# Casting DMAs for q and k, four units ahead, and transposes as pairs of 64x64 tiles, in an attention and spectral-mixing kernel

## The chip, the cores and the metric

The kernel runs on one core of one Trainium2 chip. The metric is the device time of one execution in microseconds (us), and lower is better. Before the change it was 457.25 us (median of 3 runs, 457.01 to 457.38). PE is the matmul engine (PEld are its weight loads), DVE the vector engine, ACT the scalar engine and POOL the GpSimd engine. SP is the engine that issues plain DMAs here. A run over 1.5% above the fastest of its kernel counts as slow.

## The reference

```python
# attention: 8 batches, 8 heads, 576 tokens, head size 64, window 128, ALiBi bias
scores = q @ k.T / sqrt(64);  mask = (rel >= 0) & (rel < 128)      # rel = query position - key position
scores = where(mask, scores - slope[h] * |rel|, -1e9)
x = softmax(scores) @ v                    # heads side by side: x is [8, 576, 512]
# spectral mixing
X = rfft(x, axis=1)[:, :64]                # 64 modes are kept
Y[m] = X[m] @ (w_r[m] + 1j * w_i[m])       # 2 x 64 matrices of 512 x 512 fp32, 134 MB in all
u = x + irfft(Y, n=576)
out = u + relu(u @ w_ch)                   # [8, 576, 512] fp32
```

## The kernel before

Attention runs as 16 units of four heads. It is a software pipeline: one `STAGE` list fixes, for each engine, the order of the instructions of several units. After every second unit the forward transform ("spectrum") of one batch follows. The 128 mixing matrices of 1 MB are a long DMA stream. Some are loaded as bf16 by casting GpSimd DMAs while attention still runs (`AHEAD`, `LATER`), the others as fp32 by SP. After the last matrix, the inverse transform and the output remain.

```python
TPP = 9
STAGE = (
    ("exp", 1, 0), ("score", 0, 0), ("exp", 0, 0), ("value", 0, 1), ("spectrum", None, 2),
    ("cast", "v", 0), ("score", 2, 0), ("channels", None, 2), ("transpose", "k", -1),
    ("cast", "k", -2), ("exp", 2, 0), ("norm", 0, 1), ("cast", "q", -3), ("score", 3, 0),
    ("mask", 1, 0), ("value", 1, 1), ("evacuate", "k", -1), ("mask", 0, 0), ("exp", 3, 0),
    ("transpose", "q", -2), ("evacuate", "q", -2), ("score", 1, -1), ("norm", 1, 1),
)
# ... in load(u, w): v by three SP DMAs with rows of 512 B; q and k with rows of 2304 B:
            t = self.raw[w][:, u % 2]
            nc.sync.dma_start(
                out=t.rearrange("p e j d -> p e (j d)"),
                in_=src.rearrange("(e h) (p j) d -> (h p) e (j d)", h=2, j=TPP))
# ... in cast(u, w): DVE makes bf16 of it
            dst = self.mid.tile([P, TPP, 2, D], BF16, tag=w, name=w)
            nc.vector.tensor_copy(dst.rearrange("p j e d -> p e j d"), src)
        self.load(w, u + 2)
# ... in transpose(u, w)
        for j in range(TPP):
            nc.tensor.transpose(tp[:, j], src[:, j].rearrange("p e d -> p (e d)"), self.ident)
# ... in evacuate(u, w): PSUM to SBUF
        (self.nc.vector.tensor_copy if u < 2 and w == "q" else self.nc.scalar.copy)(
            dst.rearrange("q h (p j) -> q h p j", j=TPP), ...)
# ... in value(u, e): one PSUM buffer for the unnormalized output
        av = self.ps.tile([P, 2, 512], FP32, tag="av", bufs=1)     # (cut: the last one has another)
# ... in norm(u, e): DVE frees it
        nc.vector.reciprocal(rec, tiles[:, :, :, D])
        nc.vector.tensor_tensor(out=self.x[...], in0=tiles[...], in1=rec..., op=ALU.mult)
# ... the early weights, one stage after another, gated on that stage's x
    AHEAD = {0: 1, 1: 1, 2: 1, 4: 1, 5: 1, 7: 1, 8: 1, 10: 1, 11: 1, 12: 1, 13: 3, 14: 1}
    LATER = {14: 3, 15: 3}
    EARLY, NWA, NWB, AGAIN = 14, 6, 2, 8
```

The softmax here doesn't subtract the row's maximum and nothing guards it: scores larger than these inputs give would overflow.

Of the kernel before, what the change touches and what calls it, by code (L numbers as in the profile page):

```python
# [10 lines left out]
FP32 = mybir.dt.float32  # L11
BF16 = mybir.dt.bfloat16
# [8 lines left out]
P = 128  # L21
D = 64
# [5 lines left out]
FULL = 4  # L28
TAIL = 64

TPP = 9

W = D + 2

# [3 lines left out]
STAGE = (  # L38
    ("exp", 1, 0), ("score", 0, 0), ("exp", 0, 0), ("value", 0, 1), ("spectrum", None, 2),
    ("cast", "v", 0), ("score", 2, 0), ("channels", None, 2), ("transpose", "k", -1),  # L40
    ("cast", "k", -2), ("exp", 2, 0), ("norm", 0, 1), ("cast", "q", -3), ("score", 3, 0),
    ("mask", 1, 0), ("value", 1, 1), ("evacuate", "k", -1), ("mask", 0, 0), ("exp", 3, 0),
    ("transpose", "q", -2), ("evacuate", "q", -2), ("score", 1, -1), ("norm", 1, 1),
)
# [2 lines left out]
class _Scratch:  # L47


    def __init__(self, ap):  # L50
        self.ap, self.used, self.tags = ap, 0, {}
# [55 lines left out]
class _Attention:  # L107


    def __init__(self, tc, ctx, q, k, v, consts, x, XC, raw):  # L110
        self.tc, self.nc = tc, tc.nc
        self.q, self.k, self.v = q, k, v
        self.ident, self.F, self.FT = consts
        self.x, self.XC = x, XC
        B, H, S, _ = q.shape
        self.S, self.NG = S, H // 4
        self.units = [(b, g) for b in range(B) for g in range(self.NG)]
        self.raw = raw
        self.mid = ctx.enter_context(tc.tile_pool(name="amid", bufs=2))
        self.ps = ctx.enter_context(tc.tile_pool(name="aps", bufs=1, space=PSUM))  # L120
        fix = ctx.enter_context(tc.tile_pool(name="afix", bufs=1))
        self.table = fix.tile([P, H, 2, 2 * P], BF16, name="mask")
        self.bias = fix.tile([P, H, 2, 2 * P], BF16, name="bias")
        self.vb = [fix.tile([P, 2, 4, 2, 2 * W], BF16, name=f"vb{i}") for i in range(2)]
        self.vt = [fix.tile([P, 4, 2, W], BF16, name=f"vt{i}") for i in range(2)]
        self.qkT = [fix.tile([P, 2, 2, (FULL + 1) * P], BF16, name=f"qkT{i}") for i in range(2)]
        self.att = [fix.tile([P, FULL * 8 * P + 64], BF16, name=f"att{i}") for i in range(2)]
        self.loaded, self.casted, self.open = {}, {}, {}

    def fixtures(self, i):  # L130
        nc = self.nc
# [66 lines left out]
    def load(self, w, u):  # L198
        nc = self.nc
        if u >= len(self.units):  # L200
            return
        b, g = self.units[u]
        hs = slice(4 * g, 4 * g + 4)
        if w == "v":
            t = self.raw[w][:, u % 2]
            sv = self.v[b, hs]
            for pair in range(2):
                nc.sync.dma_start(
                    out=t[:, pair],
                    in_=sv[:, 2 * pair * P : 2 * (pair + 1) * P].rearrange(  # L210
                        "h (p j) d -> p h (j d)", j=2),
                )
            nc.sync.dma_start(
                out=t[64:96, 2],
                in_=sv[:, FULL * P :].rearrange("h (p j) d -> p h (j d)", j=2),
            )
        else:
            t = self.raw[w][:, u % 2]
            src = (self.q, self.k)["qk".index(w)][b, hs]
            nc.sync.dma_start(  # L220
                out=t.rearrange("p e j d -> p e (j d)"),
                in_=src.rearrange("(e h) (p j) d -> (h p) e (j d)", h=2, j=TPP),
            )
        self.loaded[w, u] = t

    def cast(self, u, w):

        nc = self.nc
        src = self.loaded.pop((w, u))
        if w == "v":  # L230
            src = src.rearrange("p s h (j d) -> p s h j d", j=2)
            for half in range(2):
                row = slice(64 * half, 64 * half + 64)
                nc.vector.tensor_copy(  # L234
                    self.vb[u % 2][row, :, :, :, W * half : W * half + D], src[row, :2])
            nc.vector.tensor_copy(self.vt[u % 2][64:96, :, :, :D], src[64:96, 2])
        else:
            dst = self.mid.tile([P, TPP, 2, D], BF16, tag=w, name=w)
            nc.vector.tensor_copy(dst.rearrange("p j e d -> p e j d"), src)  # L239
            self.casted[u, w] = dst  # L240
        self.load(w, u + 2)

    def transpose(self, u, w):
        nc = self.nc
        src = self.casted.pop((u, w))
        if (u, w) == (0, "k"):
            tp = self.ps.tile([P, TPP, P], BF16, tag="sc", bufs=2, name="tp")
        else:
            tp = self.ps.tile([P, TPP, P], BF16, tag="tp", name="tp")
        for j in range(TPP):  # L250
            nc.tensor.transpose(tp[:, j], src[:, j].rearrange("p e d -> p (e d)"), self.ident)  # L251
        self.open[w, u] = tp

    def evacuate(self, u, w):
        tp = self.open.pop((w, u))
        dst = self.qkT[u % 2][:, "qk".index(w), :, : self.S]
        (self.nc.vector.tensor_copy if u < 2 and w == "q" else self.nc.scalar.copy)(  # L257
            dst.rearrange("q h (p j) -> q h p j", j=TPP),
            tp.rearrange("q j (h p) -> q h p j", h=2),
        )  # L260
# [137 lines left out]
def kernel(  # L398
# [10 lines left out]
    nc = tc.nc  # L409
    ctx.enter_context(tc.manual_schedule(engines=ALL | {SP}))  # L410
    B, H, S, _ = q.shape
    NM, DM, _ = moe_w_r.shape
    AHEAD = {0: 1, 1: 1, 2: 1, 4: 1, 5: 1, 7: 1, 8: 1, 10: 1, 11: 1, 12: 1, 13: 3, 14: 1}
    LATER = {14: 3, 15: 3}
    EARLY, NWA, NWB, AGAIN = 14, 6, 2, 8
    HM = NM // 2

    const = ctx.enter_context(tc.tile_pool(name="const", bufs=1))
# [6 lines left out]
    norm = const.tile([P, 1], FP32, name="norm")  # L425
# [3 lines left out]
        tc.tile_pool(name="w1", bufs=EARLY, side="right", reuse_waits="tile")  # L429
    )  # L430
    rawpool = actx1.enter_context(tc.tile_pool(name="raw", bufs=1, side="right"))
    raw = {w: rawpool.tile([P, 2, 2, TPP, D], FP32, name=w + "r") for w in "qk"}
    raw["v"] = rawpool.tile([P, 2, 3, 4, 2 * D], FP32, name="vr")
    spare = [raw[w][:, i].rearrange("p e j d -> p (e j d)") for w in "qk" for i in range(2)]
    vflat = raw["v"].rearrange("p u s h d -> p (u s h d)")
    spare += [vflat[:, 2 * DM * i :] for i in range(3)]
    spare = [t[:, : 2 * DM].bitcast(BF16).rearrange("p (a e) -> p a e", a=4) for t in spare]
    wq, homes, todo_w, again = {}, {}, list(range(2 * NM)), []

    def load_w(n, pool, bf16, chosen=None):  # L440


        for i in ([i for i in todo_w if i not in again][:n] if chosen is None else chosen):
            todo_w.remove(i)
            src = (moe_w_r, moe_w_i)[i % 2][i // 2].rearrange("(p a) e -> p a e", a=4)
            homes[i] = pool
            if bf16:
                t = spare.pop(0) if pool is None else pool.tile([P, 4, DM], BF16, tag="w", name="w")
                nc.gpsimd.dma_start(out=t, in_=src)
                wq[i] = [t[:, a] for a in range(4)]  # L450
            else:
                t = pool.tile([P, 4, DM], FP32, tag="w", name="w")
                nc.sync.dma_start(out=t, in_=src)
                wq[i] = [t[:, a].bitcast(BF16)[:, 1::2] for a in range(4)]

    with ExitStack() as actx:
        at = _Attention(tc, actx, q, k, v, (ident, F, FT), x, XC, raw)
        n = len(at.units)
        for w, u in (("q", 0), ("k", 0), ("q", 1), ("k", 1), ("v", 0), ("v", 1)):
            at.load(w, u)  # L460
        done = set()

        def run(name, arg, u):
            if 0 <= u < n and (name, arg, u) not in done:
                done.add((name, arg, u))
                getattr(at, name)(u, arg)
# [14 lines left out]
        next(table, None)  # L481
        at.fixtures(1)
        nc.gpsimd.memset(XC[:, 4 * NC * NM :], 0.0)
        run("cast", "q", 0)
        run("transpose", "q", 0)
        run("cast", "k", 0)
        run("transpose", "k", 0)
        run("evacuate", "q", 0)
        for h in (1, 3):
# [2 lines left out]
        run("score", 1, 0)  # L492
        for h in (0, 2, 1, 3):
            at.offset(h)
        run("cast", "q", 1)
        run("transpose", "q", 1)
        run("evacuate", "q", 1)
        run("score", 0, 0)
# [1 line left out]
        for h in (0, 2):  # L500
            at.decay(h)
        run("exp", 0, 0)
        run("cast", "k", 1)
        run("cast", "v", 0)
        side = {0: [(at.offset, 4), (at.offset, 6), (at.decay, 5), (at.offset, 5), (at.decay, 7),
                    (at.offset, 7), (at.decay, 4), (at.decay, 6)]}
# [1 line left out]
        for stage in range(min(lags), n + max(lags)):  # L508
            for name, arg, lag in STAGE:
                run(name, arg, stage - lag)  # L510
                if name in ("transpose", "exp") and side.get(stage):
                    for _ in range(1 + (name == "transpose")):
                        fn, h = side[stage].pop(0)
                        fn(h)
            if stage == 3:
                at.inverse_table()
            if stage in AHEAD:
                if stage:
                    b, g = at.units[stage - 1]
                    nc.gpsimd.tensor_copy(gate[:1, :1], x[:1, b, 0, 256 * g : 256 * g + 1])  # L520
                load_w(AHEAD[stage], early, True)
            if stage in LATER:
                load_w(LATER[stage], None, True)

    with ExitStack() as mctx:
# [115 lines left out]
        for g in range(NM // 4):  # L641
            acc = ps.tile([P, DM], FP32, tag="acc", bufs=2, name="acc")
            for i in range(8):
                m, ri = 4 * g + i // 2, i % 2
                w = wq[2 * m + ri]
# [9 lines left out]
                k = 8 * g + i  # L655
# [165 lines left out]
```

## Time and profile before

| what | before |
|---|---|
| time | 457.25 us |
| time of two units (spectrum to spectrum) in steady attention | 13.4 us |
| busy in such a stretch of 13.3 us | PE 12.5, DVE 12.7, ACT 12.7 us |
| last exp of attention starts | 124.3 us |
| last weight packet starts | 412.3 us |
| DMA holes up to 400 us | 3.5 us, 2.1 of them in the first 15 us |

A DMA hole is counted from the trace's packet records: whenever fewer than 16 packets are in flight, the missing share of 16 is lost time. The records do not say which of the 16 DMA engines carries a packet, so this count can only miss idle time, not invent it.

The page of the kernel before: its 40-slice rows for the DMA engines' busy tenths and their GB/s, its two large DMA queues (packets, MB, share of the engines' time), and the shares of the chain of waits that ended last.

```profile
DMA  8999999999999999999999999999999999990598
GB/s 280 324 332 309 303 264 314 312 290 254 212 303 316 311 314 314 344 399 424 422 418 422 423 421 419 420 421 422 420 420 419 421 421 419 420 373 4 219 332 276
q1 hardware_dynamic: 47280, 142.62, 81.3%
q0 software_dynamic: 4560, 15.21, 16.7%
DMA 53%; PE 25%; DVE 12%; ACT 4%; issue 3%; POOL 1%; ACTq 0%; DVEq 0%; POOLq 0%
```

The DMA engines are full from the first slice to the last weight. The GB/s of attention are lower than the 420 of the weight stream because its packets are small (by the prediction's fit of the packet records, an estimate, one of 512 B takes 29 ns and one of 8192 B 311) and because a casting DMA is counted by the bytes it writes (on the page 512 KB for a mixing matrix loaded by GpSimd, 1024 KB for one loaded by SP).

The table of windows of the kernel before, for two stretches of two units each. Columns: start and end, length, then busy us (and instructions) of each engine, granted clock, DMA share, GB/s.

```profile
core 0: us, PE busy (x) PEld busy (x) DVE busy (x) ACT busy (x) POOL busy (x), PEclk, DMA share, GB/s
54.40:67.70 13.30, 12.54 (x231) 9.67 (x229) 12.66 (x23) 12.72 (x15) 1.05 (x2) 1.00 0.99 255
67.70:81.10 13.40, 12.67 (x243) 9.79 (x240) 12.38 (x24) 12.73 (x15) 2.15 (x4) 1.00 1.09 308
```

Three compute engines are about 95% busy in the same stretch in which the DMA engines are full.

### The profile page before, as it was taken

What the parts mean: (1) busy time and instruction counts of PE and PEld (TensorE: products, weight loads), DVE (VectorE), ACT (ScalarE), POOL (GpSimd) and SP (SyncE); (2) the same over time, 40 slices, a digit from 0 to 9 for tenths busy, and PEclk for the clock granted to TensorE, in tenths of its full rate; (3) what the DMA queues carried; (4) which work ended last, traced back from release to release, by engine and by line L of the source; (5) the groups of instructions that cost most, each with busy time, mean ns of one, the idle gap of its engine ahead of it and who ended that gap; (6) DMA issues with size and microseconds to landing.
All of it is one profiled execution on the core that took longest, in us unless ns stands there. A gap on an engine that the chain in (4) does not pass through costs nothing.

```text
span 457.1 us, 7826 instructions
## 1 busy us (share of the span) xinstructions
PE 359.5 (79%) x3292; PEld 189.4 (41%) x3292; DVE 173.3 (38%) x314; ACT 154.3 (34%) x191; POOL 54.5 (12%) x86
## 2 busy tenths in 40 slices
PE   4787999999876545667566788998989788987892
PEld 3466776777653212222222243443333343433230
DVE  7889699998732101010010151211120211203674
ACT  5868799999800000000000011221111111104671
POOL 8510001012311100000000000000000000000561
PEclk9889899999999788555777799999999999999997
DMA  8999999999999999999999999999999999990598
GB/s 280 324 332 309 303 264 314 312 290 254 212 303 316 311 314 314 344 399 424 422 418 422 423 421 419 420 421 422 420 420 419 421 421 419 420 373 4 219 332 276
DMA packets 51874, 158.31 MB, mean 346 GB/s; under 512 B 3712, under 2 KB 22656, under 8 KB 39040
## 3 DMA queue, kind: packets, MB, share of 16 engines
q1 hardware_dynamic: 47280, 142.62, 81.3%
q0 software_dynamic: 4560, 15.21, 16.7%
q8 instruction: 25, 0.41, 0.4%
q14 instruction: 9, 0.07, 0.0%
HBM read 163.58 MB, written 9.44 MB: 378 GB/s over the span
## 4 chain that ended last, share of the span: by engine, by line
DMA 53%; PE 25%; DVE 12%; ACT 4%; issue 3%; POOL 1%; ACTq 0%; DVEq 0%; POOLq 0%
DMA w<-in_moe_w_i_dram 32%; DMA w<-in_moe_w_r_dram 12%; DMA vr<-in_moe_w_i_dram 7%; PE acc L648 7%; PE av L332 3%; PE my L623 2%; DVE vb L234 2%; DVE x L348 2%; DMA qr<-in_q_dram 2%; DVE att L306 2%; PE tp L251 1%; DVE q L239 1%; PE yy L752 1%; PE xt L369 1%; PE warm L636 1%
## 5 line engine op out<-in xcount | busy, mean ns | idle before, releaser
L648 PE MATMUL acc<-w,XC 128*32 128x512 bf16 x488 | 143.6, 448 | 55.0 <-DMA w<-in_moe_w_r_dram 33.2
L648 PEld LDWEIGHTS <-XC 128*32 128x32 bf16 x512 | 59.7, 140 | 130.5 <-issue 98.8
L295 ACT ACTIVATE att<-sc 128x1024 bf16<-128x1024 f32 x64 | 64.1, 1032 | 8.9 <-PE sc L285 8.9
L629 ACT CAST XW<-my 128x512 bf16<-128x512 f32 x36 | 21.1, 585 | 110.2 <-PE my L587 110.2
L733 POOL TENSOR_TENSOR r<-r,x 128x1024 f32<-128x1024 f32 x8 | 17.1, 2132 | 272.7 <-ACT r L731 272.6
L571 ACT CAST ZW<-zw 128x512 bf16<-128x512 f32 x4 | 2.3, 585 | 135.6 <-PE zw L566 135.6
L543 DVE TENSOR_SCALAR yq<-acc 128x512 bf16<-128x512 f32 x14 | 9.7, 690 | 101.2 <-PE acc L648 101.2
L611 DVE COPY xT<-tr 128x1024 bf16<-128x1024 bf16 x18 | 12.4, 691 | 90.6 <-PE tr L609 90.6
L332 PE MATMUL av<-vb,att 128*128 128x132 bf16 (+1 forms) x576 | 39.2, 220 | 5.5 <-DVE x L348 3.6
L332 PEld LDWEIGHTS <-att 128*128 128x128 bf16 x704 | 37.4, 100 | 11.0 <-DVE x L348 8.0
L623 PE MATMUL my<-wch,xT 128*64 128x512 bf16 x288 | 37.9, 385 | 0.8 <-DVE xT L611 0.8
L257 ACT COPY qkT<-tp 128x1152 bf16<-128x1152 bf16 x30 | 33.5, 1116 | 2.8 <-PE tp L251 2.2
L285 PE MATMUL sc<-qkT 64*64 64x256 bf16 (+2 forms) x640 | 25.7, 269 | 2.1 <-ACT qkT L257 1.2
L348 DVE TENSOR_TENSOR x<-av,rec 128x640 bf16<-128x640 f32 x32 | 26.4, 824 | 1.1
L766 DVE TENSOR_TENSOR o<-yy,r 128x1024 f32<-128x1024 f32 (+1 forms) x20 | 21.7, 1114 | 8.0 <-PE yy L752 4.2
L285 PEld LDWEIGHTS <-qkT 64*64 64x64 bf16 x640 | 14.8, 111 | 19.2 <-issue 16.2
L623 PEld LDWEIGHTS <-xT 128*64 128x64 bf16 x288 | 13.2, 109 | 22.6 <-issue 9.3
L234 DVE CAST vb<-vr 64x1024 bf16<-64x1024 f32 x32 | 22.3, 697 | 0.2
L272 PE MATMUL sc<-bias,ident 128*128 128x512 bf16 x64 | 20.4, 402 | 1.4 <-ACT att L295 1.4
L306 DVE TENSOR_TENSOR att<-att,mask 128x1024 bf16<-128x1024 bf16 x32 | 20.6, 684 | 0.0
L731 ACT ACTIVATE r<-mm 128x1024 f32<-128x1024 f32 (+1 forms) x19 | 17.7, 977 | 6.7 <-PE mm L587 6.5
L251 PE MATMUL tp<-ident,q 128*128 128x128 bf16 x144 | 11.9, 234 | 5.4 <-DVE q L239 5.4
(105 smaller groups left out, 326.0 us busy)
## 6 DMA issues: line engine op xcount, KB each, us to landing
w<-in_moe_w_i_dram SPq DMA_DIRECT2D x54, 1024.0 KB, 18.4
w<-in_moe_w_r_dram SPq DMA_DIRECT2D x46, 1024.0 KB, 18.5
qr<-in_q_dram SPq DMA_DIRECT2D x16, 576.0 KB, 8.6
kr<-in_k_dram SPq DMA_DIRECT2D x16, 576.0 KB, 9.0
vr<-in_v_dram SPq DMA_DIRECT2D x32, 256.0 KB, 7.7
w<-in_moe_w_r_dram POOLq DMA_DIRECT2D x15, 512.0 KB, 23.5
out_dram<-o SPq DMA_DIRECT2D x15, 512.0 KB, 4.3
w<-in_moe_w_i_dram POOLq DMA_DIRECT2D x7, 512.0 KB, 8.3
```

The lines of the kernel that those rows point to most:

```text
L234: nc.vector.tensor_copy(self.vb[u % 2][row, :, :, :, W * half : W * half + D], src[row, :2])
L257: (self.nc.vector.tensor_copy if u < 2 and w == "q" else self.nc.scalar.copy)(dst.rearrange("q h (p j) -> q h p j", j=TPP), tp.rearrange(" ...
L272: nc.tensor.matmul(sc[:, e], lhsT=self.ident, rhs=self.bias[:, hv].rearrange("p j n -> p (j n)"), start=True, stop=False, skip_group_check ...
L285: nc.tensor.matmul(sc[64 * half : 64 * half + 64, e, j * 256 + c0 : j * 256 + c0 + n], lhsT=qkT[row, 1, h, k0 + j : k0 + P : 2], rhs=qkT[r ...
L295: self.nc.scalar.activation(self.att[u % 2][:, kt * 8 * P : (kt + 1) * 8 * P], sc.rearrange("p e n -> p (e n)"), AF.Exp, scale=1.0 / math. ...
L306: nc.vector.tensor_tensor(out=rows, in0=rows, in1=self.table[:, heads], op=ALU.mult)
L332: nc.tensor.matmul(bank[:, qt * W : qt * W + rhs[j].shape[1]], lhsT=att[:, o : o + P], rhs=rhs[j], start=(n == 0 and j == 0), stop=(n == l ...
L348: nc.vector.tensor_tensor(out=self.x[:, b, :, cs].rearrange("p t (h d) -> p h t d", h=2), in0=tiles[:, :, :, :D], in1=rec.unsqueeze(-1).br ...
L623: nc.tensor.matmul(mm[ROWS[half]], lhsT=lhsT, rhs=wch[:, dt], start=(dt == 0), stop=False, skip_group_check=True,)
L629: nc.scalar.copy(XW[:, j, n], mm)
L648: nc.tensor.matmul(acc[32 * (i // 2) : 32 * (i // 2) + 32], lhsT=XC[:, c0 : c0 + 31 * NM + 1 : NM], rhs=w[a], start=(ri == 0 and a == 0), ...
L766: nc.vector.tensor_tensor(out=o[:, c], in0=yy[:, c], in1=r[:, c], op=ALU.add)
```

## The change: its intent, and the diff

Casting DMAs deliver bf16, so DVE need not cast q and k. A row of 4608 B holds 18 tokens instead of 9, which halves the number of packets. Loading four units ahead should hide the loads' latency (on the page before, 8.6 and 9.0 us in the median from the issue of a q or k load to its landing). With 64 channels per row, the transposes become 36 tiles of 64x64, in pairs of one tile from partitions 0 to 63 and one from 64 to 127. DVE gets back part of the freed time by evacuating q of even units. The saved buffer space holds two more early weights.

```diff
-TPP = 9
+TPP = 18
+DEPTH = 4
@@ STAGE
-    ("cast", "k", -2), ("exp", 2, 0), ("norm", 0, 1), ("cast", "q", -3), ("score", 3, 0),
+    ("exp", 2, 0), ("norm", 0, 1), ("score", 3, 0),
@@ load
-            t = self.raw[w][:, u % 2]
-            nc.sync.dma_start(
-                out=t.rearrange("p e j d -> p e (j d)"),
-                in_=src.rearrange("(e h) (p j) d -> (h p) e (j d)", h=2, j=TPP),
+            t = self.raw[w][:, u % DEPTH]
+            nc.gpsimd.dma_start(
+                out=t.rearrange("p j d -> p (j d)"),
+                in_=src.rearrange("h (p j) d -> (h p) (j d)", j=TPP),
             )
@@ transpose
         for j in range(TPP):
-            nc.tensor.transpose(tp[:, j], src[:, j].rearrange("p e d -> p (e d)"), self.ident)
+            for e in range(2):
+                row = slice(64 * e, 64 * e + 64)
+                nc.tensor.transpose(tp[row, j], src[row, j], self.ident[row, row])
+        self.load(w, u + DEPTH)
@@ evacuate
-        (self.nc.vector.tensor_copy if u < 2 and w == "q" else self.nc.scalar.copy)(
+        (self.nc.vector.tensor_copy if w == "q" and (u < 2 or u % 2 == 0) else self.nc.scalar.copy)(
@@ schedule of the early weights
-    AHEAD = {0: 1, 1: 1, 2: 1, 4: 1, 5: 1, 7: 1, 8: 1, 10: 1, 11: 1, 12: 1, 13: 3, 14: 1}
-    LATER = {14: 3, 15: 3}
-    EARLY, NWA, NWB, AGAIN = 14, 6, 2, 8
+    AHEAD = {0: 1, 1: 1, 2: 1, 3: 1, 4: 1, 5: 1, 6: 1, 7: 1, 8: 1, 9: 1, 10: 1, 11: 2, 12: 2, 13: 1}
+    LATER = {13: 2, 14: 2, 15: 3}
+    EARLY, NWA, NWB, AGAIN = 16, 5, 2, 8
@@ first loads
-        for w, u in (("q", 0), ("k", 0), ("q", 1), ("k", 1), ("v", 0), ("v", 1)):
+        for w, u in [(w, u) for u in range(DEPTH) for w in "qkv" if w != "v" or u < 2]:
             at.load(w, u)
# cut: the removed casts, the shapes of the buffers, the spare slots made from them
```

More of the change, by code (lines that the diff above doesn't have):

```diff
@@ L127, in __init__ @@
         self.att = [fix.tile([P, FULL * 8 * P + 64], BF16, name=f"att{i}") for i in range(2)]
-        self.loaded, self.casted, self.open = {}, {}, {}
+        self.loaded, self.open = {}, {}
     def fixtures(self, i):
@@ L228, in cast @@
         nc = self.nc
-        src = self.loaded.pop((w, u))
-        if w == "v":
-            src = src.rearrange("p s h (j d) -> p s h j d", j=2)
-            for half in range(2):
-                row = slice(64 * half, 64 * half + 64)
-                nc.vector.tensor_copy(
-                    self.vb[u % 2][row, :, :, :, W * half : W * half + D], src[row, :2])
-            nc.vector.tensor_copy(self.vt[u % 2][64:96, :, :, :D], src[64:96, 2])
-        else:
-            dst = self.mid.tile([P, TPP, 2, D], BF16, tag=w, name=w)
-            nc.vector.tensor_copy(dst.rearrange("p j e d -> p e j d"), src)
-            self.casted[u, w] = dst
+        src = self.loaded.pop((w, u)).rearrange("p s h (j d) -> p s h j d", j=2)
+        for half in range(2):
+            row = slice(64 * half, 64 * half + 64)
+            nc.vector.tensor_copy(
+                self.vb[u % 2][row, :, :, :, W * half : W * half + D], src[row, :2])
+        nc.vector.tensor_copy(self.vt[u % 2][64:96, :, :, :D], src[64:96, 2])
         self.load(w, u + 2)
@@ L244, in transpose @@
         nc = self.nc
-        src = self.casted.pop((u, w))
+        src = self.loaded.pop((w, u))
         if (u, w) == (0, "k"):
-            tp = self.ps.tile([P, TPP, P], BF16, tag="sc", bufs=2, name="tp")
+            tp = self.ps.tile([P, TPP, D], BF16, tag="sc", bufs=2, name="tp")
         else:
-            tp = self.ps.tile([P, TPP, P], BF16, tag="tp", name="tp")
+            tp = self.ps.tile([P, TPP, D], BF16, tag="tp", name="tp")
         for j in range(TPP):
-            nc.tensor.transpose(tp[:, j], src[:, j].rearrange("p e d -> p (e d)"), self.ident)
+            for e in range(2):
+                row = slice(64 * e, 64 * e + 64)
+                nc.tensor.transpose(tp[row, j], src[row, j], self.ident[row, row])
         self.open[w, u] = tp
+        self.load(w, u + DEPTH)
     def evacuate(self, u, w):
@@ L431 @@
     rawpool = actx1.enter_context(tc.tile_pool(name="raw", bufs=1, side="right"))
-    raw = {w: rawpool.tile([P, 2, 2, TPP, D], FP32, name=w + "r") for w in "qk"}
+    raw = {w: rawpool.tile([P, DEPTH, TPP, D], BF16, name=w + "r") for w in "qk"}
     raw["v"] = rawpool.tile([P, 2, 3, 4, 2 * D], FP32, name="vr")
-    spare = [raw[w][:, i].rearrange("p e j d -> p (e j d)") for w in "qk" for i in range(2)]
+    spare = [raw[w][:, 2 * i : 2 * i + 2].rearrange("p u j d -> p (u j d)")[:, : 4 * DM]
+             for i in range(2) for w in "qk"]
     vflat = raw["v"].rearrange("p u s h d -> p (u s h d)")
-    spare += [vflat[:, 2 * DM * i :] for i in range(3)]
-    spare = [t[:, : 2 * DM].bitcast(BF16).rearrange("p (a e) -> p a e", a=4) for t in spare]
+    spare += [vflat[:, 2 * DM * i : 2 * DM * (i + 1)].bitcast(BF16) for i in range(3)]
+    spare = [t.rearrange("p (a e) -> p a e", a=4) for t in spare]
     wq, homes, todo_w, again = {}, {}, list(range(2 * NM)), []
@@ L483 @@
         nc.gpsimd.memset(XC[:, 4 * NC * NM :], 0.0)
-        run("cast", "q", 0)
         run("transpose", "q", 0)
-        run("cast", "k", 0)
         run("transpose", "k", 0)
@@ L494 @@
             at.offset(h)
-        run("cast", "q", 1)
         run("transpose", "q", 1)
@@ L502 @@
         run("exp", 0, 0)
-        run("cast", "k", 1)
         run("cast", "v", 0)
```

## The prediction

> **What bounds the kernel now.** The 16 DMA engines. In the trace's packet records at least 16 packets are in flight nearly always from 6 to 409 us; only 50-60 us (92% filled) and 100-120 us (96 to 99%) have small holes, 1.3 us together. The chain of waits is 53% DMA. After 200 us the engines move 420 GB/s; in attention (60-113 us) source bytes come at about 358 GB/s, because packets are small. Compute there is close behind: in two-unit stretches of 13.38 us (table of windows) PE is busy 12.6, ACT 12.7, DVE 12.4. The last weight lands at 412 us; the 45 us after it are untouched. So only fewer engine-seconds of DMA, or different DMA holes, move the end.
>
> **Cost per packet.** A fit (an estimate) of packet counts in saturated 4 us stretches gives 29 ns for 512 B (v), 96 for 2304 B (q, k), 311 for 8192 B (weights), 309 for a casting packet of 8192 B source. Cost follows source bytes; casting is free; a packet has 11-12 ns of its own. [...]
>
> **What the change does.**
> 1. q and k: 8192 packets of 96 ns become 4096 of an estimated 180 ns (4608 B source): 49.1 to 46.1 us on 16 engines. Gain 3 us, maybe 4.
> 2. A weight in nearly every stage fills the later holes: gain 1 us.
> 3. Start: eight casting loads (0.53 us of GpSimd each, the first 1.2, as weight issues show) now precede GpSimd's 16.6 us of setup. Identity, tables and masks come 4.4 us later, and unit 4's loads wait for the end of setup, at 22 us, with data 3 us later (before: weight issued 17.3, first packet 20.5). The work queued at the start is an estimated 16 us, so the engines run dry from about 18 us, with only v of unit 2 in between: loss 3 to 4 us.
> 4. DVE loses 32 casts of 0.76 us and gains 7 evacuations of 1.36, which ACT loses (1.12 each). PE swaps 9 transposes 56 ns apart for 36 of 64 columns; 66-column neighbours start 29 ns apart, so 0.55 us if pairs overlap like the score matmuls (3 ns apart), 1.1 if not, against 0.5. All off the critical path: a unit with its weight needs an estimated 7.4 us of DMA, above the 6.7 of compute.
> 5. Weight slots 16+7 bf16 and 5+2 fp32, against 14+6 and 6+2: seven still queue 17 us of DMA. Neutral.
>
> **Sum:** -3.4 - 1.0 + 3.5: **456.3 us**, range 451.5 to 460.5. Faster by over 2%: 0.07; within 2%: 0.88; slower by over 2%: 0.05.
>
> **What would show it.** 4096 packets of 2304 B on the software queue, instead of 8192 on the hardware one; a DMA hole between 18 and 25 us and none later; transposes waiting for qr and kr, DVE and ACT with new idle; still 420 GB/s after 200 us and the 45 us tail; first exp and forward table 3 to 4 us later.
>
> **What would make it wrong.** If the start hole is filled, or casting packets cost well under 180 ns: 3 to 5 us faster. If paired transposes make PE the limit (over 7.4 us a unit), or GpSimd, which waits in order for transposes, gates and earlier landings, issues loads late: holes in attention, 0.5 to 1 us per unit slower. If the smaller fp32 pool drains DMA where early slots are re-used: a few us more.

The sum, -3.4 - 1.0 + 3.5 = -0.9 us, takes the 457.25 us of before to about 456.3. A packet's own 11 to 12 ns are an estimate from the fit's figures: 96 ns for 2304 B and 311 ns for 8192 B leave 11.9 ns for no bytes at all. That GpSimd waits in order is seen in the trace before, where it waited 86.8 us in 11 pieces for the norms that gate the weights.

## More of the kernel before

Part of the chain of waits of the kernel before between 66 and 96 us (start, duration, what):

```profile
75.38 0.76 DVE k L239
76.30 0.82 DVE x L348
77.12 0.67 DVE q L239
77.79 1.20 DVE att L306 x2
79.16 0.83 DVE x L348
80.04 1.23 PE av L332 x20
```

The norm (`x`, 0.83 us) frees the one PSUM buffer (PSUM is the memory that PE writes to) called `av`, and the next value matmuls follow at once (at 80.04 us; the norm ends at 79.99). Apart from the norm's own reciprocal, which needs the value matmuls of its unit, nothing that stands before `x` on DVE in this stretch waits for PE.

## The result, and the profile after

The time rose to 470.59 us (median of 4 runs, 469.29 to 471.78), against 457.13 us of the kernel before in the same rounds (455.38 to 457.38, 4 runs). The ratio is 1.0302, with a 95% interval of 1.0264 to 1.034: slower by 3%. Ratios here and below are the mean time of one kernel's fast runs over that of the other's fast runs of the same rounds, so they are not quite the ratio of the quoted medians.

| what | before | after |
|---|---|---|
| two units, spectrum to spectrum, in turn | 16.9, 13.4, 13.4, 13.4, 13.4, 13.3, 8.8 us | 27.1, 16.3, 16.3, 17.0, 17.0, 14.8, 9.0 us |
| first exp, last exp start | 10.3, 124.3 us | 15.0, 150.6 us |
| DMA holes up to 400 us | 3.5 us | 14.3 us |
| of these from 15 to 25, from 40 to 80, from 80 to 160 us | 0.0, 0.8, 0.5 | 2.5, 6.2, 3.3 |
| last weight packet | 412.3 us | 425.2 us |
| from the last weight to the end | 45 us | 43 us |

The page of the kernel after, the same lines:

```profile
DMA  8899898999999999999999999999999999990498
GB/s 186 178 210 221 167 203 162 218 227 172 238 197 213 303 314 304 318 350 409 422 421 421 420 421 422 420 420 422 420 419 422 422 417 423 420 415 37 155 343 310
q1 hardware_dynamic: 38144, 120.60, 66.0%
q0 software_dynamic: 9600, 26.22, 29.9%
DMA 49%; PE 30%; issue 8%; DVE 7%; ACT 3%; POOL 2%; ACTq 0%; DVEq 0%; POOLq 0%
```

The busy digits hardly moved, and the weight stream after attention still runs at 420 GB/s. The chain has moved: PE and "issue" have grown, DMA has shrunk. The last weight comes 12.9 us later, and this is the whole loss (the tail after it is even 1.5 us shorter). The holes grew by 10.9 us, which is most of it.

The table of windows of the kernel after, for two stretches of two units (columns as before):

```profile
65.70:82.00 16.30, 13.01 (x334) 10.74 (x337) 10.54 (x18) 11.69 (x13) 4.17 (x8) 0.96 0.87 177
98.30:115.30 17.00, 13.79 (x336) 11.45 (x339) 11.40 (x21) 12.15 (x14) 3.63 (x7) 0.90 0.98 190
```

DVE and ACT do have less to do than before, and PE 0.3 to 1.3 us more, but the stretches are 3 to 3.6 us longer: every compute engine now waits about 3 us or more. Attention had become bound by waits between engines, while its DMA queue ran dry. The granted clock of PE is also lower where PE waits (0.91 in the mean from 60 to 120 us, against 1.00 before). The question is which waits.

**First finding: v arrives late.** The chain of waits of the kernel after, between 25 and 50 us:

```profile
25.94 0.45 DVE x L347
26.38 21.49 DMA vr<-in_v_dram
47.90 0.42 DVE vt L236
48.35 0.23 DVE rec L346
48.60 0.84 DVE x L347
49.48 2.14 PE av L331 x24
```

One load of v took 21.49 us from its issue to its landing. The view of the DMA engines for the window of 26 to 48 us, with packets, MB and share of engine time of each queue:

```profile
DMA packets 3320, 4.82 MB, mean 219 GB/s; under 512 B 238, under 2 KB 1920, under 8 KB 3317
q0 software_dynamic: 1575, 3.91, 91.0%
q1 hardware_dynamic: 1742, 0.86, 17.4%
```

Two queues had work: GpSimd's (q0) with q, k and weights, and SP's (q1) with v alone. They moved about the same number of packets, 1575 and 1742. But a packet of v is 512 B, and one of the other queue holds 4608 or 8192 B of source. In the packet records of each 2 us between 30 and 44 us, where both queues had work throughout, there are likewise 112 to 169 data packets of v and 109 to 151 of the casting queue. From 44 to 46 us the casting queue has only 79, and v at once has 303. So while both queues had work, v got about every second packet of data, but over the window only 17.4% of the engines' time. (On SP's queue here every record with data is a row of 512 B.) By what rule an engine picks between the queues the trace does not show; these are counts. Four units of q and k plus a weight per stage kept the casting queue supplied. Before, q and k stood on the same queue as v and had smaller packets (2304 B).

**Second finding: DVE waits in front of the norm.** The chain of waits of the kernel after, at 60 us:

```profile
60.62 0.62 PE tp L249 x32
61.35 1.36 DVE qkT L256
62.87 0.84 DVE x L347
63.75 2.16 PE av L331 x20
65.91 1.72 PE xt L368 x20
```

PE transposes q, DVE evacuates it in 1.36 us, and only then comes the norm `x`, which frees the single `av` buffer for PE. In the trace DVE works in the order of `STAGE`, where the evacuation (61.35 us) stands before the norm (62.87 us). On ACT, which evacuated q before, the norm did not stand behind it. The same evacuation stands in the chain at 78.6, 111.6 and 128.6 us as well. The table of waits of the kernel after (what waits, for what: total us, times, longest):

```profile
POOL kr L222 <- PE tp L249: 35.6, 9, 6.8
PE av L331 <- DVE x L347: 18.9, 9, 6.9
DVE qkT L256 <- PE tp L249: 14.1, 7, 2.2
```

The third line is the evacuation waiting for PE (7 times). The second is PE waiting for the norm; its longest wait, 6.9 us, is the one for v of the first finding. The second line in the kernel before:

```profile
PE av L332 <- DVE x L348: 3.6, 7, 1.2
```

The first line is how the wait reaches DMA: the loads of k are issued one unit at a time, when PE has read the old buffer. Late compute therefore issues loads late, and the engines run dry.

**Third finding: pauses that no semaphore explains.** From 60 to 140 us the chain of the kernel after also has pieces called "issue", one of them 1.73 us long at 94.64 us. In the kernel before, there is no such pause inside a group of matmuls, apart from short gaps of 0.3 to 0.56 us at the same places in both kernels, which are not counted below.

### The profile page after: what moved, and what is told of

Its sections match the earlier page's. It is cut to its first block, busy times and chain, and to the rows that moved or that the text cites. A ratio compares the mean times of both kernels' runs of the same rounds, so it can differ in the third digit from the quotient of the medians.

```text
span 468.6 us, 9492 instructions
## 1 busy us (share of the span) xinstructions
PE 353.9 (76%) x4119; PEld 196.3 (42%) x4156; DVE 161.7 (34%) x289; ACT 147.1 (31%) x184; POOL 71.9 (15%) x123
## 4 chain that ended last, share of the span: by engine, by line
DMA 49%; PE 30%; issue 8%; DVE 7%; ACT 3%; POOL 2%; ACTq 0%; DVEq 0%; POOLq 0%
DMA w<-in_moe_w_r_dram 24%; DMA w<-in_moe_w_i_dram 20%; PE acc L644 9%; PE av L331 5%; DMA vr<-in_v_dram 5%; PE tp L249 3%; PE sc L284 2%; PE xt L368 2%; PE my L619 1%; DVE qkT L256 1%; DVE o L762 1%; DVE x L347 1%; PE warm L632 1%; PE sc L271 1%; PE yy L748 1%
## 5 line engine op out<-in xcount | busy, mean ns | idle before, releaser
L644 PE MATMUL acc<-w,XC 128*32 128x512 bf16 x484 | 137.0, 434 | 55.0 <-DMA w<-in_moe_w_r_dram 34.5
L625 ACT CAST XW<-my 128x512 bf16<-128x512 f32 x36 | 21.1, 586 | 109.7 <-PE my L583 109.7
L331 PE MATMUL av<-vb,att 128*128 128x132 bf16 (+1 forms) x576 | 40.0, 222 | 20.2 <-DVE x L347 18.9
L256 ACT COPY qkT<-tp 128x1152 bf16<-128x1152 bf16 x23 | 25.6, 1114 | 12.4 <-PE tp L249 12.4
L284 PEld LDWEIGHTS <-qkT 64*64 64x64 bf16 x640 | 15.6, 108 | 22.2 <-issue 17.8
L727 ACT ACTIVATE r<-mm 128x1024 f32<-128x1024 f32 (+1 forms) x19 | 17.7, 977 | 6.7 <-PE mm L583 6.5
L256 DVE COPY qkT<-tp 128x1152 bf16<-128x1152 bf16 x9 | 12.1, 1348 | 14.1 <-PE tp L249 14.1
L271 PE MATMUL sc<-bias,ident 128*128 128x512 bf16 x34 | 14.1, 426 | 2.4 <-ACT att L294 2.3
## 6 DMA issues: line engine op xcount, KB each, us to landing
w<-in_moe_w_r_dram SPq DMA_DIRECT2D x52, 1024.0 KB, 16.3
```

Of the source, the lines that this page charges most:

```text
L256: (self.nc.vector.tensor_copy if w == "q" and (u < 2 or u % 2 == 0) else self.nc.scalar.copy)(dst.rearrange("q h (p j) -> q h p j", j=TPP) ...
L271: nc.tensor.matmul(sc[:, e], lhsT=self.ident, rhs=self.bias[:, hv].rearrange("p j n -> p (j n)"), start=True, stop=False, skip_group_check ...
L284: nc.tensor.matmul(sc[64 * half : 64 * half + 64, e, j * 256 + c0 : j * 256 + c0 + n], lhsT=qkT[row, 1, h, k0 + j : k0 + P : 2], rhs=qkT[r ...
L331: nc.tensor.matmul(bank[:, qt * W : qt * W + rhs[j].shape[1]], lhsT=att[:, o : o + P], rhs=rhs[j], start=(n == 0 and j == 0), stop=(n == l ...
L625: nc.scalar.copy(XW[:, j, n], mm)
L644: nc.tensor.matmul(acc[32 * (i // 2) : 32 * (i // 2) + 32], lhsT=XC[:, c0 : c0 + 31 * NM + 1 : NM], rhs=w[a], start=(ri == 0 and a == 0), ...
```

## The experiments

Eleven kernels ran. The first four undo one part of the changed kernel each, or two; the next two add one part to the kernel before; the last five tell the remaining causes apart. All outputs were correct. Line numbers in the profiles shift by a line or two between the kernels. "Pauses" below is the summed time in attention in which PE stood still inside a group of matmuls without a wait for any semaphore, from the trace's instruction records, counted from the start of the matmul before to the start of the one after (so each includes some 0.2 us of work); all these pauses ended 1.2 to 1.6 us after a 16 KB packet of the instruction queue had landed.

### e1_evac_act: q evacuated by ACT again

```diff
-        (self.nc.vector.tensor_copy if w == "q" and (u < 2 or u % 2 == 0) else self.nc.scalar.copy)(
+        (self.nc.vector.tensor_copy if w == "q" and u < 2 else self.nc.scalar.copy)(
```

> The changed kernel with one part undone: q of units 2, 4, ... 14 is evacuated by ScalarE again (units 0 and 1 stay on VectorE). Theory B (the evacuation on VectorE stands ahead of the norm of the unit before, so the single value buffer comes free late and PE waits): two units take 13.4 to 14.5 us in place of 16.9 between 60 and 130 us, the DMA holes after 60 us (about 5.5 us in the changed kernel) shrink to under 1.5, and the time falls by 4 to 7 us, to 464 to 467. Theory A (v is starved by the queue of casting loads): the stall of about 8 us near 37-46 us stays, and the time falls by at most 2 us. Theory C (paired transposes are too dear for PE): no change, as PE does the same.

Measured: 466.96 us (465.2 to 468.11), ratio 1.0217 [1.0181, 1.0252], so 3.6 us less than the changed kernel. The two-unit times were 25.4, 17.0, 16.7, 13.8, 18.6, 15.5 and 9.0 us, not the steady short ones that the theory asked for. The pauses without a semaphore rose from 2.95 us to 13.1 us. The evacuation matters, but as soon as this wait was gone, another took much of its place.

### e2_v_pool: the later loads of v on GpSimd's queue

```diff
-                nc.sync.dma_start(          # both places of v's load
+                (nc.sync if u < 2 else nc.gpsimd).dma_start(
```

> The changed kernel with the v loads of units 2 and up issued by GpSimd as well, in one queue with q, k and weights (uncast, same packets). Theory A [...]: VectorE's wait for v near 37-46 us (8.3 us) vanishes, with it the DMA hole at 50-60 us (3.3 us), and the time falls by 3 to 8 us. Theory B (order of the evacuation on VectorE): two units still take 16.5 to 17 us after 60 us and the time falls by at most 4 us. If GpSimd's in-order issue is the limit (theory D), three more issues per unit make it slower.

Measured: 464.79 us (463.67 to 466.63), ratio 1.0176 [1.0142, 1.0211], 5.8 us less. The hole from 40 to 60 us is gone (0.0 instead of 3.3 us), and the first two-unit time fell from 27.1 to 19.5 us. The six loads of v for units 3 and 4 land 7.7 to 10.1 us after their issue, against 12.6 to 21.5 us in the changed kernel and 7.5 to 10.8 us before it: v no longer falls behind on a queue of its own beside one of large packets. But this run changed a second thing, which its expectation ("same packets") had not foreseen. In the packet records, v on this queue stands as records of 4096 B. They can be told from the weights' records of the same size by their duration (mostly 140 to 240 ns, against 320 to 340), and a fit that does so (an estimate) gives about 195 ns for one, against 219 to 232 ns for eight of 512 B. Over 2016 such records on 16 engines that is an estimated 3 to 5 us of DMA time saved. The holes up to 400 us shrank by only 1.3 us (14.3 to 13.0). So the end of v's starvation is shown, but how much of the 5.8 us is due to it is not: a large part can be cheaper packets. The others stayed at 16.3 to 17.5 us, with PE still waiting for the norm.

### e3_both: both of these

```diff
# the edits of e1_evac_act and e2_v_pool together
```

> e1 and e2 together. If A and B are the two causes, nothing but the start hole is left: 458 to 462 us, DMA filled over 97% from 25 to 150 us, two units in 14 to 15 us (limited by loads). If the paired transposes or the casting packets (theory C) cost time, it stays above 464.

Measured: 461.38 us (459.2 to 463.23), ratio 1.0082 [1.0032, 1.0133]. The gain of 9.2 us is about the sum of the two (3.6 and 5.8). PE's wait for the norm fell from 18.9 to 1.2 us. But the two-unit times were still 21.1, 17.8, 17.7, 14.0, 17.8 and 13.8 us. A part of the chain of waits of this kernel:

```profile
64.30 0.59 PE tp L249 x30
64.89 2.88 issue
67.77 0.22 PE tp L249 x2
```

PE stops after 30 of 36 transposes of one group. The chain shows no other engine in this pause of 2.88 us. A packet of the instruction queue, 16384 B, started at 64.99 us and took 1.25 us; the transposes went on 1.53 us after it had landed. The pauses of this kernel sum to 14.3 us; the longest is 3.07 us. Counted in PE instructions (matmuls and weight loads), the pauses stand whole multiples of 256 apart: exactly so in e5_many_instr below (256 and 11 x 256), and to within 4 here, where the trace lacks some records. The count of packets of the instruction queue gives about as many instructions to each (32 packets for some 8314, 25 on the page of the kernel before for 6586, 28 in e7_both_wide for 7162); such 256 are called a block below. So the pauses lie one or more whole blocks apart and end after a packet has landed: from this the author infers that PE stands at the end of a block and waits for the next. No record shows that wait itself. This brought up a new theory: PE's own instruction stream, now longer by 27 transposes per q or k, does not come fast enough. The program has 8314 PE instructions, against 6586 before the change.

### e4_start: a shorter start, in the changed kernel

```diff
-        for w, u in [(w, u) for u in range(DEPTH) for w in "qkv" if w != "v" or u < 2]:
-            at.load(w, u)
+        for u in range(2):
+            at.load("v", u)
...      # q and k of units 0 and 1 are issued after the forward table's first POOL work,
...      # those of units 2 and 3 before fixtures(0); fixtures(1) moves behind the first transposes
```

> The changed kernel with its start reordered: GpSimd makes the identity and the index tables first, then loads units 0 and 1, then the distances, then loads units 2 and 3; q and k of unit 4 are issued before the second set of memsets. Start theory (4 to 5 us of casting issues ahead of GpSimd's setup delay everything and open a DMA hole at 15-25 us of 2.5 us): first exp 3 to 4 us earlier, hole under 0.7 us, time falls by 2 to 3 us. If A and B hold alone, the saved time at the start is lost again in the stall for v, and the time falls by under 1 us.

Measured: 470.04 us, ratio 1.0287 [1.0238, 1.0336]: nothing gained. The start itself worked: the hole from 15 to 25 us went from 2.5 to 0.0 us and the first exp from 15.0 to 12.6 us. But the holes from 40 to 80 us grew from 6.2 to 8.8 us. This fits an attention that is bound by its own waits: DMA work done earlier then only means that the queue is empty for longer later.

### e5_many_instr and e6_few_instr: more instructions, or the same PE time in few, in the kernel before

The first adds 27 transposes of 64x64 to each group of the kernel before (their results are overwritten). The second does the 9 transposes twice.

```diff
# e5_many_instr
+        for i in range(27):
+            row = slice(64 * (i % 2), 64 * (i % 2) + 64)
+            nc.tensor.transpose(tp[row, i // 2 % TPP, :D], src[row, i // 2 % TPP, 0], self.ident[row, row])
# e6_few_instr
+        for j in range(TPP):
+            nc.tensor.transpose(tp[:, j], src[:, j].rearrange("p e d -> p (e d)"), self.ident)
```

> The kernel before, with 27 extra transposes of 64x64 in front of the nine of each transpose call (their result is overwritten, so the output is right): PE executes as many instructions as in the changed kernel (8314 in the program, from 6586), in some 0.5 us of extra PE time per call. Theory D ([...] the PE stalls of e1_evac_act and e3_both end 1.2 to 1.6 us after such a block has landed): PE gaps of this kind of at least 5 us in all between 20 us and the end of attention (before: none), and two units take 15.5 us or more in place of 13.4. Rival (PE time, not instructions): no such gaps, two units in 14 to 15.4 us, the same as in e6_few_instr.

> The control: the kernel before with the nine 128x128 transposes of each call done twice (0.5 us of extra PE time per call, as much as in e5_many_instr, but a third of its extra instructions; 7162 in the program). Theory D: PE gaps after a block's landing under 2 us in all, two units in 14 to 15 us, faster than e5_many_instr. Rival: the same as e5_many_instr within 1 us of total time.

(Cut from the first: theory D's clause on how blocks would arrive and why one would come late, a conjecture then; "such a block" is a 16384 B packet of the instruction queue.)

Measured: 471.78 us, ratio 1.0313 [1.0279, 1.0347] for many, and 468.69 us (6 runs), ratio 1.0262 [1.0232, 1.0292] for few. Two units took 15.5 and 15.2 us, against 13.4. The pauses were only 2.7 us with many and none with few: the theory's forecast of 5 us or more was a miss. Two things differ from e3_both, the time per block and the packets of q and k, which are half as large here. As for the first: in this form the extra instructions come with extra PE time, so a new block of 256 is needed less often: an estimate from the counts and times is every 5.7 us here and every 5.2 in e3_both without its pauses, against 7.1 in the kernel before.

The control was the surprise. About 2.0 us more PE work per two units, with no other edit, made two units 1.8 us longer and the kernel 11.5 us longer. PE time in attention was hardly off the critical path even before the change.

### e7_both_wide: e3_both with 18 transposes instead of 36

The rows go back to 9 tokens, still cast by GpSimd DMAs and four units ahead. Each transpose takes all 128 partitions and 64 columns.

```diff
-TPP = 18
+TPP = 9
-                in_=src.rearrange("h (p j) d -> (h p) (j d)", j=TPP),
+                in_=src.rearrange("(e h) (p j) d -> (h p) e (j d)", h=2, j=TPP),
-                row = slice(64 * e, 64 * e + 64)
-                nc.tensor.transpose(tp[row, j], src[row, j], self.ident[row, row])
+                nc.tensor.transpose(tp[64 * e : 64 * e + 64, j], src[:, e, j], self.ident)
# cut: the shapes that go with it
```

> e3_both with q and k loaded as half rows (2.3 KB source, two per partition, still casting, still four units ahead) and transposed by 18 tiles of 128x64 in place of 36 of 64x64 (7162 PE instructions in place of 8314; 8192 q and k packets in place of 4096, 3 us more of DMA time). Theory D: the PE stalls after a block's landing (about 15 us in all in e3_both) fall under 4 us, two units take 14 to 15.5 us, attention ends 5 us or more earlier than in e3_both; the total gains 2 to 4 us net of the dearer packets, 457 to 460. Without theory D it is 2 to 4 us slower than e3_both.

Measured: 456.18 us (455.08 to 457.3), ratio 0.9976 [0.9946, 1.0005]. The pauses are gone (0), two units take 13.7 us throughout after the first 18.1, and there is no DMA hole after 25 us. Against e3_both this is 5.2 us, more than the forecast of 2 to 4. By the trace one group takes PE 0.474 us instead of 0.563. With four groups in two units that is 0.4 us, too little for the 4 us by which e3_both's long stretches exceed 13.7. PE's granted clock from 60 to 120 us is back at 1.00.

This run does not separate the number of instructions from the size of the packets, since the rows became half as long too. A count of PE's instructions in the traces (an estimate) lets one look at both. From the start of one block to the landing of the next it takes at most 4.4 us here, 5.4 in e5_many_instr and 6.7 in e3_both. So a block also came sooner here. Whether the shorter rows (2304 B of source a packet instead of 4608) are the reason was not shown. Many instructions with short rows and no extra PE time were not run.

### e8_all_wide: e7_both_wide with the start of e4_start

```diff
# the edit of e4_start on e7_both_wide
```

> e7_both_wide with the reordered start of e4_start. With the other three causes gone, the start hole should count at last (it gained nothing in e4_start, because the time was lost again in the waits for v): 2 to 4 us faster than e7_both_wide, 454 to 457, and DMA holes of under 5 us in all up to 400 us. If the start does not matter, the same as e7_both_wide within 1 us.

Measured: 453.04 us (452.54 to 453.27), ratio 0.9905 [0.9882, 0.9929]. This version beats the kernel before by 1%, and the changed one by about 4%. The same edit that gained nothing in e4_start is worth 3.1 us here. The page of this kernel, the DMA rows and the chain:

```profile
DMA  8999999999999999999999999999999999980598
GB/s 170 196 201 237 245 234 244 235 242 242 237 220 317 315 317 315 351 404 424 422 422 420 421 420 420 420 422 418 422 420 420 420 422 418 421 335 4 207 340 293
DMA 54%; PE 26%; issue 6%; POOL 6%; ACT 4%; DVE 3%; ACTq 0%; DVEq 0%; SPq 0%; POOLq 0%
```

The holes sum to 3.9 us, as before the change (3.5), and the last weight comes at 407.3 us, 5.0 us before that of the kernel before. A fit says where that can come from (an estimate, with v's and the weights' records told apart as in e2_v_pool): a casting q or k packet of 2304 B source costs about 93 ns here (96 in e11_wide_v_sp, where v is on the other queue), and the same bytes on SP's queue cost 96 to 98 ns before, so 8192 of them save 0 to 3 us. The joined records of v save another 3 to 5 us. So much of the gain over the kernel before can be due to v's larger packets, which are no part of the change, and not to casting.

### e9_no_weights: e3_both with no early weights until late

All 16 early weights are loaded at stage 13, so that during attention the DMA engines have little to do. This was one run with a profile; its state is unknown, so only what happens inside attention is read from it.

```diff
-    AHEAD = {0: 1, 1: 1, 2: 1, 3: 1, 4: 1, 5: 1, 6: 1, 7: 1, 8: 1, 9: 1, 10: 1, 11: 2, 12: 2, 13: 1}
+    AHEAD = {13: 16}
```

> e3_both with all sixteen early weights loaded at stage 13 in place of one or two per stage, so that the DMA engines are far from full in attention; PE's instructions stay the same (8314 in the program). It must be slower in total (about 30 us of weight loads come later). Theory D [...]: PE stalls inside a group of matmuls after a block's landing fall from about 14 us in all (e3_both) to under 3 us, and two units take about 14.0 us between 60 and 110 us (e3_both: 17.8, 17.7, 14.0, 17.8). If the number of instructions alone makes PE stall, whatever the DMA engines do, the stalls stay at 10 us or more.

Measured: 487.9 us, long as expected, since the DMA engines were left idle (33.5 us of holes). Two units took 20.7, 13.8, 14.6, 13.8, 13.8 and 13.8 us, and the pauses fell from 14.3 to about 3.2 us (just above the forecast of less than 3). It has the same PE instructions and the same transposes as e3_both. So the 36 small transposes are not too slow for PE in themselves: with rows of this length most of the pauses went when the DMA engines were less full (DMA share from 60 to 120 us 0.71, against 0.98 in e3_both), and many instructions alone are not enough for them. In what way full DMA engines delay a block was not shown.

### e10_wide_dve: e7_both_wide with DVE evacuating even units' q

```diff
-        (self.nc.vector.tensor_copy if w == "q" and u < 2 else self.nc.scalar.copy)(
+        (self.nc.vector.tensor_copy if w == "q" and (u < 2 or u % 2 == 0) else self.nc.scalar.copy)(
```

> e7_both_wide with one part of the change put back alone: q of units 2, 4, ... 14 evacuated by VectorE. Theory B (that evacuation waits for PE's transposes and stands ahead of the norm, so the value buffer comes free about 2 us late every second unit, then the next unit pays again): two units take 15.5 to 17 us in place of 13.7, PE waits about 2 us for the norm (line of x) in every second unit, total 3 to 7 us above e7_both_wide (459 to 463). If B had only looked guilty because of the other waits: within 1 us of e7_both_wide.

Measured: 465.53 us (461.92 to 468.39), ratio 1.0156 [1.0101, 1.021], 9 us more than e7_both_wide and more than expected. Its line in the table of waits:

```profile
PE av L330 <- DVE x L346: 14.9, 10, 1.9
```

The same wait in e7_both_wide:

```profile
PE av L330 <- DVE x L346: 2.0, 2, 1.2
```

Two units took 16.8 to 16.9 us, with no pauses at all, and holes came back to 12.9 us. This is the second finding alone. In the 36-transpose form the same edit was worth only 3.4 to 3.6 us, because there the pauses took the place of the wait (14.3 us of them in e3_both).

### e11_wide_v_sp: e7_both_wide with v on SP's queue again

```diff
-                (nc.sync if u < 2 else nc.gpsimd).dma_start(
+                nc.sync.dma_start(
```

> e7_both_wide with v back on the SP queue for all units, all else kept. Theory A [...]: one v load of an early unit takes 12 us or more from issue to landing, VectorE waits 4 to 9 us for it once, the total is 2 to 6 us above e7_both_wide (458 to 462). Otherwise within 1 us of e7_both_wide.

Measured: the four runs were 456.95, 461.82, 466.1 and 471.37 us. The last two count as slow, so the two fast runs alone give a ratio of 1.0047 [0.9978, 1.0116]. The time is inconclusive. The profile fell on the 471.37 us run, which counts as slow. It shows the wait itself, but as a slow run it is not used to explain a time:

```profile
DVE vb L234 <- DMA vr<-in_v_dram: 30.9, 7, 11.0
```

Seven waits for v, up to 11.0 us, against 8.0 us in eight waits, up to 2.5, in e7_both_wide. That v starves on a queue of its own rests on the landing times of the changed kernel, e2_v_pool and e3_both. How much it costs in this form stays open: the kernel varies from run to run.

## Why the prediction was wrong, point by point

**Right: what bounds the kernel.** Time followed the last weight in all profiles of fast runs, and the last weight followed mainly the DMA holes. The 45 us after it hardly changed.

**Right: the costs by themselves.** A casting packet of 4608 B costs 183 ns (fit), predicted 180; two casting ones of 2304 B at 91 to 96 ns (fits of the later runs) would cost 182 to 192, so the longer rows saved at most about 9 ns. A group of 36 paired transposes takes 0.563 us from first to last, predicted 0.55; the tiles of a pair start 3 to 4 ns apart. The start was late by 4.7 us (predicted 3 to 4) and its hole was 2.5 us (predicted a loss of 3 to 4). The weight slots were neutral: there is no hole from 160 to 400 us.

**Wrong: step 4, "All off the critical path: a unit with its weight needs an estimated 7.4 us of DMA, above the 6.7 of compute."** This is the step that failed. The 6.7 us were half of the measured 13.4 of the kernel before, and were carried over as if the compute of a unit were only the sum of its instructions. In the changed kernel a unit took 8.2 to 8.5 us, above DMA's 7.4. Three things did it, none of which is mainly more work for an engine:

1. The evacuation on DVE stands in program order before the norm and waits there for PE, so PE waits for the `av` buffer. The prediction counted its 1.36 us only as busy time of an engine that had some to spare. Shown by e1_evac_act and e2_v_pool against e3_both, and alone by e10_wide_dve (+9 us).
2. v stays behind on its own queue and got about one 512 B packet per 4.6 or 8 KB packet of the others (112 to 169 against 109 to 151 in each 2 us). The prediction added up packets per queue and did not ask how queues share. Shown by the counts from 30 to 44 us and by the landing times in e2_v_pool. Its worth is not shown: e2_v_pool gained 5.8 us, of which an estimated 3 to 5 can be v's cheaper packets.
3. PE pauses at the ends of blocks of its own instructions. That 27 more instructions per group use up blocks faster than they arrive beside full DMA engines is inference. Hidden in the changed kernel (2.95 us of pauses), since PE waits there anyway; 14.3 us of pauses once the first two are gone (e3_both). That these are waits for blocks is inferred from their spacing of 256 instructions and from the packets that landed 1.2 to 1.6 us before each one's end. e9_no_weights, where emptier DMA engines remove most, shows the part of DMA; e7_both_wide, where they are gone, has fewer instructions and also shorter packets.

**Wrong: step 2, "A weight in nearly every stage fills the later holes."** Weights are issued by stage, so they come late when compute is late. Holes grew from 3.5 to 14.3 us, 9.5 of them in the times from 40 to 160 us that this step was to fill.

**The listed risk.** The prediction named "0.5 to 1 us per unit slower" if PE became the limit or GpSimd issued loads late, and gave 5% to slower by over 2%. The consequence was of this kind (1.4 to 1.8 us per unit), and late issues on GpSimd were part of it (its loads of k waited 35.6 us for PE, in 9 waits). The cause of the lateness was not among those named.

**The sum.** In ratios to the kernel before: from the changed kernel's 1.0302, undoing the first two causes takes 0.022 (about 10 us, v's cheaper packets included), and going to 18 transposes with short rows takes 0.011 (5 us). That leaves e7_both_wide at 456.18 us, next to the predicted 456.3. The agreement is largely luck, since e7_both_wide has other rows, cheaper v packets and a start hole of 5.0 us. The start order takes another 0.007 (3 us), down to 453.04 us.

**Open.** The holes explain 10.9 of the 12.9 us by which the last weight moved, and cheaper q and k packets should have brought back 2 to 3; the difference, 4 to 5 us, is not located. The packet records have no engine number, so idle time on single engines cannot be seen. Why a block of instructions takes so long to come was not measured step by step, and the number of instructions was not separated from the length of the packets. How the engines choose between queues is not shown; the records give counts alone. PE's granted clock was 0.90 to 0.91 from 60 to 120 us in the kernels where DVE evacuates (the changed one, e2_v_pool, e10_wide_dve), 0.95 in e3_both, and 1.00 in e7_both_wide and e8_all_wide. It went with PE's waits; whether it added to their cost was not separated.

## What to carry to other kernels

When engines and DMA are all near 95% busy, an operation moved to an engine with spare time must be judged by where it stands in that engine's order: ask what it waits for, and who needs what stands behind it (here an evacuation that stood before the norm cost 9 us in e10_wide_dve). When part of the traffic moves to another DMA queue, look at what stays on the old one, because the share of a queue can go by packets and not by bytes, as it did here (1742 and 1575 packets, but 17.4% of the engines' time against 91.0%). When a transfer moves to another queue, look in the records whether its packets changed too (v's went from 512 to 4096 B in e2_v_pool). Count instructions as well as their time when one large matmul is split into many small ones beside full DMA engines, and look for pauses at a fixed number of instructions (here multiples of 256, 14.3 us in all in e3_both).
